# Zero products in another type and number, and the first tile of x in two parts

## Chip, cores and metric

The kernel runs on one core of one Trainium2 chip. The metric is the device time of one execution in microseconds (us). The engines go by the profile's names: PE (TensorE; its weight loads are PEld), DVE (VectorE), ACT (ScalarE), POOL (GpSimd) and SP (SyncE).

## Reference

The kernel computes a recurrent attention and, on its result, a gated feed-forward layer. q, k and v have 4 batches, 8 heads, 768 steps and a head dimension of 64; the layer has 512 inputs and 1536 hidden units.

```python
gamma = 1.0 - 2.0 ** (-5.0 - np.arange(H))
for t in range(S):
    state = gamma * state + k[t] (outer) v[t]          # per batch and head
    y[t] = scale * q[t] @ state
x = y.transpose(0, 2, 1, 3).reshape(B * S, H * D)      # 3072 x 512
gate = 1.0 / (1.0 + np.exp(-(x @ w_gate)))
out = (gate * (x @ w_val)) @ w_out
```

## The kernel before, in words

The 768 steps are cut into six chunks of 128. Inside a chunk the attention is a product of scores with a causal mask of decays; between chunks a state of 64x64 per head is carried. The four batches of a chunk are two *blocks* of two batches each, so there are twelve blocks (`i`, with `j` the batch within the block). The x of one chunk, 512 tokens of four batches by 512 features, is held as `xT`: 128 partitions by four row blocks (`kk`, one for each pair of heads) by 512 columns. The feed-forward layer of a chunk is 12 groups (`n1`) of 128 hidden units: four products over `kk` with `wg`, four with `wv`, a sigmoid on ACT, a product on DVE into `hT`; then `down` products with `wo`.

The order of the work is written out by hand: each engine takes its instructions in program order. Sums are held in eight banks (`bank()`), used in turn: a new one waits until the tile eight allocations ago has been read. Loads are issued by POOL in program order, apart from the first k and q (SP and ACT). Later chunks follow a hand-written plan; the change touches none of it but the name of the x tile.

The first chunk, where the change lies, runs so:

- POOL issues the loads of k, q and v for the first chunk (line 92; k of batch 0 and q of batch 0 come by SP and ACT in fp32), then the weights: `wg` and `wv` of the first 256 hidden units in two parts each (line 79), `kk` 0 and 1 first, and so on.
- DVE writes `zero` (line 135), a tile of 128x512 in bf16, and builds tables; among them `causal` (line 140, used for the decays; written anew at line 175, by `last_constants`, as a 0/1 table that POOL reads for `maskk`, line 184, much later).
- PE does `keep_on(11)`: eleven products of `zero` with itself into a bank that nobody reads (line 416). Four more `keep_on(1)` stand between later steps of the head.
- DVE and ACT cast k and q of batch 0 to bf16 (lines 161 and 162). For each block and batch PE then transposes k and q (line 311), ACT or DVE copies them to `kqT` (line 312), PE makes the scores (line 226), DVE masks them (line 318), PE makes y of the batch (line 326, in `first_y`), and an engine evicts y from its bank into 128 columns of `xT` (line 329): ACT for the first three batches, DVE for the last.
- ACT loads the table of the sigmoid (line 447), DVE writes the second `causal`.
- PE begins the feed-forward layer with `first_parts` (line 363): gate sums of `n1` 0 and 1 over `kk` 0 and 1, then over `kk` 2 and 3, and the same for val; then groups of up to 12 products (line 354), with the two first states in between (line 340, copied by DVE at line 343, cast at line 277).

The order of the eviction and the first products is

```python
    c = (2 * i + j) * C
    eng(xT[0][:, :, c:c + C], o)
...
    for lo in (0, 2):
        for n1, u in enumerate(us):
            for kk in range(lo, lo + 2):
                nc.tensor.matmul(u, w[:, kk, n1 * 128:(n1 + 1) * 128], xT[0][:, kk], start=(kk == 0), stop=(kk == KT - 1))
```

so that every product of the layer reads a tile that all four evictions have written.

Of the kernel before, what the change touches and what calls it, by code (L numbers as in the profile page):

```python
# [8 lines left out]
F32 = mybir.dt.float32  # L9
BF16 = mybir.dt.bfloat16  # L10
AX = mybir.ActivationFunctionType
ALU = mybir.AluOpType
# [3 lines left out]
def kernel(  # L16
# [12 lines left out]
    nc = tc.nc  # L29
# [3 lines left out]
    C = 128  # L33
    NT = S // C
    NP = H // 2
    KT = D_MODEL // 128
# [6 lines left out]
    const = ctx.enter_context(tc.tile_pool(name="const", bufs=1))  # L43
    wpool = ctx.enter_context(tc.tile_pool(name="wpool", bufs=1))
    ld = ctx.enter_context(tc.tile_pool(name="ld", bufs=2))
    at = ctx.enter_context(tc.tile_pool(name="at", bufs=2))
# [38 lines left out]
    def load_out(s):  # L85
        nc.gpsimd.dma_start(out=wo[:, s * 3:(s + 1) * 3, :],
                            in_=moe_w_out.rearrange("(n p) d -> p n d", p=128)[:, s * 3:(s + 1) * 3, :])
# [43 lines left out]
    tabsk = const.tile([128, NT, 2, H], F32, name="tabsk")  # L131
    taby = const.tile([128, NP, C], F32, name="taby")
    tabz = const.tile([128, NT, 2, NP], F32, name="tabz")
    zero = const.tile([128, 512], BF16, name="zero")
    nc.vector.memset(zero, 0.0)  # L135
    nc.vector.memset(lsc, math.log(scale))
    for h in range(H):
# [36 lines left out]
    def last_constants():  # L174
        nc.vector.tensor_scalar(causal, ahead, 0.0, None, op0=ALU.is_le)
# [13 lines left out]
    xT, sc, stA, stB, y, za, zz, zb = {}, {}, {}, {}, {}, {}, {}, {}  # L189

    def bank(shape, dt=F32):
        return pf.tile(shape, dt, tag="ff", name="ff")

    def half(e):
        return slice(e * D, (e + 1) * D)
# [4 lines left out]
    def new_kqT(i):  # L200
        kqT[i] = at.tile([128, 2, 2, NP, C], BF16, tag="kqT", name="kqT", bufs=2)
# [43 lines left out]
    def intra(i, j):  # L245
        for p in range(NP):
            for e in range(2):
                st = (stA, stB)[e ^ j][i, j]
                nc.tensor.matmul(y[i, j][half(e), p, :], vs[i][:, j * H + 2 * p + e, :], st[:, p, :],  # L249
                                 start=False, stop=True, skip_group_check=True)  # L250

    def y_out(i, j):
        t = i // 2
        if t not in xT:
            xT[t] = at.tile([128, NP, 512], BF16, tag="xT", name="xT")
        c = (i % 2 * 2 + j) * C
        nc.vector.tensor_tensor(xT[t][:, :, c:c + C], y[i, j], taby, op=ALU.mult)  # L257

    def state(i):
        zz[i] = bank([128, 2, NP, D])  # L260
# [7 lines left out]
    def new_za(i):  # L268
        za[i] = at.tile([128, 2, NP, D], F32, tag="za", name="za", bufs=4)
# [9 lines left out]
    def block(old, new):  # L279
        last = new is None or new >= NPAIR - 2  # L280
        if old is not None:
            new_y(old)
            inter(old)
        for j in range(2):
            if new is not None:
                scores(new, j)
        for j in range(2):
            if old is not None:
                intra(old, j)
        if not last:  # L290
            state(new)
        for j in range(2):
            if old is not None:
                y_out(old, j)
        for j in range(2):
            if new is not None:
                mask(new, j, 0)
                mask(new, j, 1)
        if not last:
            state_sum(new)  # L300
# [6 lines left out]
    def first_transpose(i, j, which, eng):  # L307
        x = (kn[i], qn[i])[which]
        tp = bank([128, NP, C], BF16)
        for p in range(NP):  # L310
            nc.tensor.transpose(tp[:, p, :], heads(x, j, p), ident)
        eng(kqT[i][:, which, j], tp)

    def first_scores(i, j):
        scores(i, j)
        for e, st in enumerate((stA, stB)):
            st[i, j] = at.tile([128, NP, C], BF16, tag=f"st{e}", name=f"st{e}", bufs=4)
            nc.vector.tensor_tensor(st[i, j], sc[i, j][e], decay[:, e], op=ALU.mult)

    def first_y(i, j, eng):  # L320
        if 0 not in xT:
            xT[0] = at.tile([128, NP, 512], BF16, tag="xT", name="xT")
        o = bank([128, NP, C])
        for p in range(NP):
            for e, st in enumerate((stA, stB)):
                nc.tensor.matmul(o[half(e), p, :], vs[i][:, j * H + 2 * p + e, :], st[i, j][:, p, :],
                                 start=(p == 0), stop=True, skip_group_check=True)
        c = (2 * i + j) * C
        eng(xT[0][:, :, c:c + C], o)  # L329

    def first_scaled(i, j, x):
        nc.gpsimd.tensor_tensor(entry(ks[i], j), x, tabs[:, :, 0].unsqueeze(2).to_broadcast([C, H, D]), op=ALU.mult)

    def first_state(i):
        z = bank([128, 2, NP, D])
        for j in range(2):
            for p in range(NP):
                for e in range(2):
                    n = j * H + 2 * p + e
                    nc.tensor.matmul(z[half(e ^ j), j, p, :], ks[i][:, n, :], vs[i][:, n, :],  # L340
                                     start=(j == 0 and p == 0), stop=True, skip_group_check=True)
        new_za(i)
        nc.vector.tensor_copy(za[i], z)
# [5 lines left out]
    def up_part(t, w, n1s, lo=0, hi=512):  # L349
        n = hi - lo  # L350
        u = bank([128, 512])
        for i, n1 in enumerate(n1s):
            for kk in range(KT):
                nc.tensor.matmul(u[:, i * n:(i + 1) * n], w[:, kk, n1 * 128:(n1 + 1) * 128], xT[t][:, kk, lo:hi],  # L354
                                 start=(kk == 0), stop=(kk == KT - 1))
        return u[:, :len(n1s) * n]

    def first_parts(w):
        us = [bank([128, 512]) for _ in range(2)]
        for lo in (0, 2):  # L360
            for n1, u in enumerate(us):
                for kk in range(lo, lo + 2):
                    nc.tensor.matmul(u, w[:, kk, n1 * 128:(n1 + 1) * 128], xT[0][:, kk], start=(kk == 0), stop=(kk == KT - 1))  # L363
        return us

    def gate_times_val(t, n1s, lo, hi, ps):
        n = hi - lo
        if t not in hT:
            hT[t] = ffn.tile([128, NFF, 512], BF16, tag="hT", name="hT", bufs=2)
        gs = ffn.tile([128, 512], F32, tag="gs", name="gs")  # L370
        g = gs[:, :len(n1s) * n]
        nc.scalar.activation(g, ps[0], AX.Sigmoid)  # L372
        nc.vector.tensor_tensor(hT[t][:, n1s[0]:n1s[-1] + 1, lo:hi], g.rearrange("p (i n) -> p i n", n=n),  # L373
                                ps[1].rearrange("p (i n) -> p i n", n=n), op=ALU.mult)

    def up(t, n1s, lo=0, hi=512):
        gate_times_val(t, n1s, lo, hi, [up_part(t, w, n1s, lo, hi) for w in (wg, wv)])
# [35 lines left out]
    def keep_on(n):  # L413
        u = bank([128, 512])
        for _ in range(n):
            nc.tensor.matmul(u, zero[:, :128], zero, start=True, stop=True)  # L416

    act, dve = nc.scalar.copy, nc.vector.tensor_copy  # L420

    new_kqT(0)
    new_kqT(1)
    keep_on(11)
    first_transpose(0, 0, 0, dve)
    first_transpose(0, 0, 1, act)
    later_constants()
# [1 line left out]
    first_scores(0, 0)  # L429
    first_transpose(0, 1, 1, act)  # L430
    first_transpose(1, 0, 0, act)
    keep_on(1)
    first_scores(0, 1)
    first_transpose(1, 0, 1, act)
    keep_on(1)
    first_scores(1, 0)
    first_transpose(1, 1, 0, act)
    later_exps()
    first_transpose(1, 1, 1, dve)
    keep_on(1)  # L440
    first_y(0, 0, act)
    first_scores(1, 1)
    first_y(0, 1, act)
    keep_on(1)
    first_y(1, 0, act)
    first_y(1, 1, dve)
    nc.scalar.preload_act_table(AX.Sigmoid)
    last_constants()
    first_scaled(0, 0, kf)
    first_scaled(0, 1, entry(kn[0], 1))  # L450
    load_gate_val(3)
# [4 lines left out]
    for n1, ps in enumerate(zip(first_parts(wg), first_parts(wv))):  # L456
        gate_times_val(0, (n1,), 0, 512, ps)
    for n1 in (2, 4):
        gates = [up_part(0, wg, (n1 + i,)) for i in range(2)]
        for i in range(2):  # L460
            gate_times_val(0, (n1 + i,), 0, 512, (gates[i], up_part(0, wv, (n1 + i,))))
        first_state(n1 // 2 - 1)
    load_out(0)
    load_out(1)
    load_kq(2)
# [35 lines left out]
    for j in range(2):  # L501
        y_out(2, j)
# [68 lines left out]
```

## Time and profile before

| | us |
|---|---|
| median of 4 runs | 228.64 (228.54 to 230.09) |
| the profiled execution | 228.73 |
| its span, first to last instruction | 227.0 |
| PE busy in the span | 219.9 |
| POOL busy | 104.9 |
| DVE busy | 111.2 |
| ACT busy | 71.8 |
| the 15 zero products on PE | 6.4 |
| first feed-forward product starts | 15.79 |

The profile shows one execution. The span is shorter than the execution by what lies around it. Busy shares are means over the whole span; where an engine stood still is read from the chain of work that ended last and from the timeline, which lists instructions by start, with the idle time before each and what ended it.

The chain says that of the span 92% is PE, 4% POOL and 2% DMA. POOL and DMA stand in it before 14.5 us alone; after 15.79 it is PE to the last copy.

### The profile page before, as it was taken

The page shows a single profiled execution, that of the slowest core. Times are in us where ns is not written, and L with a number is a line of the kernel's source. Part 1 is how long each engine was busy: PE and PEld are TensorE (multiplying, and loading weights), DVE is VectorE, ACT ScalarE, POOL GpSimd, SP SyncE. Part 2 cuts the span into 40 slices and gives each one's busy share as a digit, 9 for nine tenths or more (in the row PEclk, how much of TensorE's full clock was granted, in tenths as well). Part 3 has the DMA queues.
Part 4 walks back from the last instruction along what each step waited for, and adds up shares of the span by engine and source line. Part 5 has one row for each costly group of instructions (what it writes and reads, how often), then busy time and mean ns, then how long its engine had stood idle before and what let it go on. Part 6 is the DMA issues. An engine that isn't in the chain of part 4 may idle for free.

```text
span 227.0 us, 4324 instructions
## 1 busy us (share of the span) xinstructions
PE 219.9 (97%) x1767; PEld 116.9 (51%) x1767; DVE 111.2 (49%) x198; ACT 71.8 (32%) x120; POOL 104.9 (46%) x127
## 2 busy tenths in 40 slices
PE   7869999999999999999999999999999999999994
PEld 2534445558888555445445445445445444444443
DVE  6753653163954776735916634904443802333301
ACT  6674232336233212332321332321433321333221
POOL 8999969999849989089900081000000000000000
PEclk9999999999999999999999999999999999999999
DMA  9999999999999999999952799012600012100022
GB/s 128 152 174 195 189 199 168 162 210 196 150 133 148 146 179 187 180 137 102 101 84 87 161 123 87 3 46 95 137 3 0 3 46 92 49 1 0 0 95 92
DMA packets 103668, 25.19 MB, mean 111 GB/s; under 512 B 92640, under 2 KB 100704, under 8 KB 103648
## 3 DMA queue, kind: packets, MB, share of 16 engines
q0 software_dynamic: 80928, 13.90, 80.8%
q1 hardware_dynamic: 21536, 10.69, 20.4%
q10 hardware_dynamic: 1184, 0.33, 0.6%
q8 instruction: 14, 0.23, 0.4%
q14 instruction: 6, 0.05, 0.1%
HBM read 28.31 MB, written 6.29 MB: 152 GB/s over the span
## 4 chain that ended last, share of the span: by engine, by line
PE 92%; POOL 4%; DMA 2%; DVE 0%; issue 0%; POOLq 0%
PE ff L354 54%; PE ff L389 27%; PE ff L249 2%; PE ff L226 2%; DMA vs<-in_v_dram 2%; PE ff L363 2%; PE ff L242 2%; POOL kn L92 1%; PE ff L402 1%; POOL qn L92 1%; POOL vs L92 1%; PE ff L264 1%; PE ff L207 1%; PE ff L340 0%; DVE xT L329 0%
## 5 line engine op out<-in xcount | busy, mean ns | idle before, releaser
L373 DVE TENSOR_TENSOR hT<-gs,ff 128x512 bf16<-128x512 f32 x72 | 49.0, 686 | 63.2 <-PE ff L354 60.2
L354 PE MATMUL ff<-xT,wg 128*128 128x512 bf16 (+1 forms) x328 | 71.7, 348 | 0.0
L354 PE MATMUL ff<-xT,wv 128*128 128x512 bf16 (+1 forms) x328 | 71.7, 348 | 0.0
L372 ACT ACTIVATE gs<-ff 128x512 f32<-128x512 f32 x72 | 42.9, 597 | 83.6 <-PE ff L354 79.0
L389 PE MATMUL ff<-wo,hT 128*128 128x512 bf16 x276 | 62.2, 379 | 0.0
L354 PEld LDWEIGHTS <-wv 128*128 128x128 bf16 x328 | 32.1, 98 | 28.5
L354 PEld LDWEIGHTS <-wg 128*128 128x128 bf16 x328 | 31.4, 98 | 27.6
L389 PEld LDWEIGHTS <-hT 128*128 128x128 bf16 x276 | 26.2, 98 | 30.8 <-DVE hT L373 0.4
L393 ACT COPY ob<-ff 128x512 f32<-128x512 f32 x23 | 13.5, 585 | 58.7 <-PE ff L389 54.7
L232 DVE TENSOR_TENSOR st<-ff,maskk 128x512 bf16<-128x512 f32 x40 | 24.8, 682 | 6.4 <-PE ff L226 6.4
L257 DVE TENSOR_TENSOR xT<-ff,taby 128x512 bf16<-128x512 f32 x20 | 12.9, 686 | 29.6 <-PE ff L249 29.6
L218 POOL TENSOR_TENSOR ks<-kn,tabsk 128x1024 bf16<-128x1024 bf16 x8 | 15.9, 1988 | 0.0
L67 POOL DMA_DIRECT2D qn<-in_q_dram x20 | 15.4, 800 | 0.9 <-DMA wv<-in_moe_w_val_dram 0.6
L67 POOL DMA_DIRECT2D kn<-in_k_dram x20 | 15.2, 780 | 0.0
L515 POOL COPY held<-kqX 128x1 bf16<-128x1 bf16 x6 | 1.2, 208 | 28.4 <-DMA kqX<-qn 28.4
L57 POOL DMA_DIRECT2D vs<-in_v_dram x10 | 12.2, 1221 | 0.0
L63 POOL DMA_DIRECT2D kn<-in_k_dram x10 | 9.5, 946 | 0.9 <-issue 0.9
L63 POOL DMA_DIRECT2D qn<-in_q_dram x10 | 9.3, 928 | 0.0
L277 DVE TENSOR_TENSOR zb<-za,tabz 128x512 bf16<-128x512 f32 x10 | 8.0, 812 | 0.2
L416 PE MATMUL ff<-zero 128*128 128x512 bf16 x15 | 6.4, 565 | 1.2 <-DVE zero L135 1.2
L249 PE MATMUL ff<-st,vs 128*64 128x128 bf16 x160 | 6.4, 222 | 0.0
L79 POOL DMA_DIRECT2D wg<-in_moe_w_gate_dram x7 | 5.7, 834 | 0.0
(73 smaller groups left out, 121.2 us busy)
## 6 DMA issues: line engine op xcount, KB each, us to landing
out_dram<-ob SPq DMA_DIRECT2D x23, 256.0 KB, 2.2
vs<-in_v_dram POOLq DMA_DIRECT2D x10, 256.0 KB, 7.0
kn<-in_k_dram POOLq DMA_DIRECT2D x13, 128.0 KB, 5.1
qn<-in_q_dram POOLq DMA_DIRECT2D x13, 128.0 KB, 5.4
wo<-in_moe_w_out_dram POOLq DMA_DIRECT2D x4, 384.0 KB, 7.8
wg<-in_moe_w_gate_dram POOLq DMA_DIRECT2D x5, 256.0 KB, 6.1
wv<-in_moe_w_val_dram POOLq DMA_DIRECT2D x5, 256.0 KB, 6.7
kn<-in_k_dram POOLq DMA_DIRECT2D x20, 64.0 KB, 5.7
```

What stands on the lines that cost most here:

```text
L57: nc.gpsimd.dma_start(out=vs[i], in_=v[2 * h:2 * h + 2, :, t * C:(t + 1) * C, :].rearrange("b h s d -> s (b h) d"))
L63: nc.gpsimd.dma_start(out=tiles[i][:, 0:H], in_=src[0])
L67: nc.gpsimd.dma_start(out=dst[:, e], in_=pairs[:, 1 - e])
L218: nc.gpsimd.tensor_tensor(ks[i], kn[i], tabsk[:, i // 2].rearrange("s j h -> s (j h)").unsqueeze(2) .to_broadcast([C, 2 * H, D]), op=ALU.mult)
L232: nc.vector.tensor_tensor(st[i, j], sc[i, j][e], maskk[:, e ^ j], op=ALU.mult)
L249: nc.tensor.matmul(y[i, j][half(e), p, :], vs[i][:, j * H + 2 * p + e, :], st[:, p, :], start=False, stop=True, skip_group_check=True)
L257: nc.vector.tensor_tensor(xT[t][:, :, c:c + C], y[i, j], taby, op=ALU.mult)
L354: nc.tensor.matmul(u[:, i * n:(i + 1) * n], w[:, kk, n1 * 128:(n1 + 1) * 128], xT[t][:, kk, lo:hi], start=(kk == 0), stop=(kk == KT - 1))
L372: nc.scalar.activation(g, ps[0], AX.Sigmoid)
L373: nc.vector.tensor_tensor(hT[t][:, n1s[0]:n1s[-1] + 1, lo:hi], g.rearrange("p (i n) -> p i n", n=n), ps[1].rearrange("p (i n) -> p i n", n ...
L389: nc.tensor.matmul(o, hT[t][:, n1, b * C:(b + 1) * C], wo[:, n1, :], start=(n1 == 0), stop=(n1 == NFF - 1))
L393: nc.scalar.copy(ob, o)
```

## The change

The zero tile becomes 128x256 in fp32. `keep_on` multiplies 256 columns instead of 512. Five such products stand where eleven did, and the four single ones are gone.

The first chunk's x is held in two tiles, one with row blocks 0 and 1, one with 2 and 3; `x_of` finds the tile. Each eviction of the first chunk is made in two halves, one for each tile. ACT makes both for the first two batches; for the last two DVE makes the first half and ACT the second. x of the later chunks stays one tile, in two buffers of its own.

`last_constants`, the second `causal`, moves from before POOL's `first_scaled` calls to behind the second `first_state`.

```diff
-    zero = const.tile([128, 512], BF16, name="zero")
+    zero = const.tile([128, 256], F32, name="zero")
...
+    def new_xT(t, n=1):
+        xT[t] = [at.tile([128, NP // n, 512], BF16, tag=f"xT{n}", name="xT", bufs=2) for _ in range(n)]
+
+    def x_of(t, kk, lo=0, hi=512):
+        per = NP // len(xT[t])
+        return xT[t][kk // per][:, kk % per, lo:hi]
...
-    def first_y(i, j, eng):
+    def first_y(i, j, engs):
         if 0 not in xT:
-            xT[0] = at.tile([128, NP, 512], BF16, tag="xT", name="xT")
+            new_xT(0, 2)
...
-        eng(xT[0][:, :, c:c + C], o)
+        for g, eng in enumerate(engs):
+            eng(xT[0][g][:, :, c:c + C], o[:, 2 * g:2 * g + 2])
...
     def keep_on(n):
         u = bank([128, 512])
         for _ in range(n):
-            nc.tensor.matmul(u, zero[:, :128], zero, start=True, stop=True)
+            nc.tensor.matmul(u[:, :256], zero[:, :128], zero, start=True, stop=True)
...
-    keep_on(11)
+    keep_on(5)
     first_transpose(0, 0, 0, dve)
...
     first_transpose(1, 0, 0, act)
-    keep_on(1)
     first_scores(0, 1)
     first_transpose(1, 0, 1, act)
-    keep_on(1)
     first_scores(1, 0)
     first_transpose(1, 1, 0, act)
     later_exps()
     first_transpose(1, 1, 1, dve)
-    keep_on(1)
-    first_y(0, 0, act)
+    first_y(0, 0, (act, act))
     first_scores(1, 1)
-    first_y(0, 1, act)
-    keep_on(1)
-    first_y(1, 0, act)
-    first_y(1, 1, dve)
+    first_y(0, 1, (act, act))
+    first_y(1, 0, (dve, act))
+    first_y(1, 1, (dve, act))
     nc.scalar.preload_act_table(AX.Sigmoid)
-    last_constants()
     first_scaled(0, 0, kf)
...
         first_state(n1 // 2 - 1)
+    last_constants()
     load_out(0)
```

The products of `up_part` and `first_parts` read `x_of(t, kk, lo, hi)` in place of `xT[t][:, kk, lo:hi]`.

## Prediction

> **What bounds the kernel now.** I read the page's busy shares first, then the chain of work that ended last, then the timeline of the first 20 us.
>
> ```profile
> PE 219.9 (97%) x1767; PEld 116.9 (51%) x1767; DVE 111.2 (49%) x198; ACT 71.8 (32%) x120; POOL 104.9 (46%) x127
> ...
> PEclk9999999999999999999999999999999999999999
> ```
>
> PE is busy in 97% of the span, at a granted clock that never drops in the records. A change can gain only where PE stands still, or lose by making PE wait or run slower. The chain says where PE stood still:
>
> ```profile
> 9.29 5.16 DMA vs<-in_v_dram
> 14.45 0.04 issue
> 14.49 0.43 PE ff L326 x8
> 14.92 0.02 issue
> 14.95 0.70 DVE xT L329
> 15.65 0.14 issue
> 15.79 3.61 PE ff L363 x16
> 19.40 3.45 PE ff L354 x16
> ```
>
> Columns: start, length, what. Up to 14.45 the end is set by GpSimd's queue of loads, whose last early one, v of batch 3, lands at 14.45; PE's own work before that is not on the chain. Then come the last y block (14.49 to 14.92), its eviction on DVE, and from 15.79 PE without a break to 223.8. So all that this change can gain lies between 14.92 and 15.79: 0.87 us. All that it can lose is a later 15.79, or slower products after it.
>
> The timeline of the head (start, length, engine, line, operation, and in brackets the idle time and what ended it):
>
> ```profile
> 1.19 4.87 PE L416 MATMUL ff<-zero 128*128 128x512 bf16 x11 [1.19 <-DVE zero L135]
> ...
> 5.62 0.62 ACT L162 CAST qn<-qf 128x512 bf16<-128x512 f32 x1 [0.54 <-DMA qf<-in_q_dram]
> 5.86 0.63 PE L311 MATMUL ff<-ident,kn 128*128 128x128 bf16 x4
> 6.29 0.52 PE L311 MATMUL ff<-ident,qn 128*128 128x128 bf16 x4
> 6.65 0.39 PE L311 MATMUL ff<-ident,kn 128*128 128x128 bf16 x4
> ...
> 7.98 4.02 DVE L318 TENSOR_TENSOR st<-ff,decay 128x512 bf16<-128x512 f32 x6 [0.33 <-ACT kqT L312]
> ...
> 12.80 1.29 DVE L318 TENSOR_TENSOR st<-ff,decay 128x512 bf16<-128x512 f32 x2 [0.47 <-PE ff L226]
> ...
> 14.95 0.69 DVE L329 CAST xT<-ff 128x512 bf16<-128x512 f32 x1 [0.85 <-PE ff L326]
> ```
>
> Two things are to be seen. The eleven zero products start every 0.42 us ((5.86 - 1.19) / 11), the ones from 15.79 every 0.22 (3.61 / 16): PE works at half rate at first, though the granted clock shows nothing of it. Four transposes take 0.63, then 0.52, then 0.39, so the rate doubles near 6.5, after 5.3 us of unbroken work. Second, beside the loads runs a chain with little slack: cast of q (ends 6.24), transposes, scores, DVE's six masks without a pause from 7.98, and the last two, which end at 14.09. The last y could start then; it waits for v until 14.45. That slack is 0.36 us.
>
> **The change part by part.**
>
> *The eviction.* Today 128x512 on DVE takes 0.69. Then DVE takes two of four row blocks, 128x256, and the first four gate products read only these. The nearest rows are the two evictions of the kernel's end (of PSUM too, but into f32):
>
> ```profile
> 222.53 0.42 DVE L409 COPY ob<-ff 128x256 f32<-128x256 f32 x1 [8.32 <-PE ff L402]
> ...
> 223.20 0.27 ACT L406 COPY ob<-ff 128x128 f32<-128x128 f32 x1 [1.40 <-PE ff L402]
> 223.87 0.29 DVE L409 COPY ob<-ff 128x128 f32<-128x128 f32 x1 [0.92 <-PE ff L402]
> ```
>
> I take 0.42, the same shape: 0.69 - 0.42 = 0.27 us saved, and PE starts at 15.52. Bounds: a half no shorter than the 128x128 row's 0.29 saves 0.40; one as long as the whole saves nothing. The hard limit is the 0.87 above. As built, ACT's half waits for DVE's half of the same bank, so the halves follow each other: ACT from about 15.42, for a length between 0.27 (128x128) and 0.58 (its 128x512 rows), by the middle to 15.8. The fifth gate product needs it at 15.52 + 4 x 0.215 = 16.38: covered by 0.5 us. Queued behind ACT's half is the Sigmoid table load (1.28, now at 14.81); it would end at 17.1, and the first sigmoid finds its bank full at about 17.0 (today 17.28). Its 0.1 us delay meets no one: gs and hT are next needed by bank reuse microseconds later. The blocks before: DVE's half of the third block runs 14.2 to 14.6, before the last is ready at 14.92, and ACT's four short copies of the first two blocks have until then (today ACT idles 0.34 before its third).
>
> *What is late next.* The weights. The first gate part (issued 10.15, 4.7 us to landing) is there at 14.9 and the second at 15.3. The second part of val lands at 17.7 and is loaded by PE at 18.15 today, 17.9 then. The next gate columns land at 18.7; PE loads them at 19.02, then 18.75. This cover is used up at 0.3 us of gain; more would be given back there. The rest has over 0.6: q of block 2 lands at 38.4 for transposes at 39.1, the third part of w_out at 40.3 for 41.1.
>
> *The four single zero products.* They stand at 8.55, 9.46, 11.26 and 13.18, each 0.38 us. Behind the first the next weight load waits 0.26 for an ACT copy; behind the others PE itself waits 0.46 for a copy, 0.29 and 0.19 for v. Taking them away gains nothing; PE only waits longer. Their four banks leave the ring of eight, which makes the reused banks older, never younger. What their going may do to PE's rate is a rival below.
>
> *The eleven become five in fp32.* No row shows an fp32 product. From below, 256 columns at the pace of the bf16 rows take 0.21 us: the five end at 2.3. From above, as if each of four bytes took a pass of its own with its weight load (151 ns here) hidden behind nothing: 4 x (0.21 + 0.15) = 1.46, and they end at 8.5. No row is nearer, so I take the middle, 0.84: end at 5.4. The point that decides is known: the transposes of k need 0.43 before those of q, which can't start before 6.29 in any case. So an end by 5.86 costs nothing, and up to 6.22 the 0.36 us of slack at v hides it. At 8.5 the cost is 2.27 us.
>
> The Trainium skill, "FP8 and Floating Point Precision", section "TensorE Precision Notes", says that true fp32 takes four passes through the array. By that my estimate would be 4 x 0.21 = 0.85 a product and the sum the same; no run here shows it yet.
>
> *The causal table.* 0.52 us of DVE moves from 15.55, where DVE then idles until 19.07, to behind the second state copy at 28.1. Queued behind it there are zb (needed on PE at 48.2) and a product hT after which DVE idles 0.84. GpSimd reads the table at 34.4, covered by 5.8 us. Zero. x of the later tiles keeps two buffers: zero.
>
> **The sum.** The profiled execution took 228.73 (span 227.0 and 1.7 around it): 228.73 - 0.27 = 228.46. It is 0.09 above the median of 228.64, so the forecast is **228.4**.
>
> **Rivals.**
>
> *PE runs at half rate when the dense products begin (slower).* Place: the gate products from 15.5. For it: the rate rose only after 5.3 us of unbroken work; in the changed kernel that work is other work, may be shorter, and is followed by a pause of about 0.4 until q comes; and the four zeros that filled the waits are gone. Without them PE has some 1.5 us of transposes and 1.5 of scores and y between 7 and 15. Against it: no pause of PE in that stretch is over 1 us. Price: if the climb takes 5.3 us again, half of it, 2.65, and about 0.35 for slower transposes, scores and y on the masks' chain after its slack: 228.4 + 3.0 = 231.4. It decides from 2.8 us at half rate on (1.4 lost).
>
> Against this change speaks a rule of "TensorE: Matmul & The Clock Gate", section "Part 4: PE-mode transpose": transposes do not count as work for the clock. Its "Part 1: The HAM clock gate" asks for a busy window of 3.4 us to speed up and an idle one to slow down. If transposes don't count, the longest pause without zeros is 2.0 us, from 5.4 to 7.5, so the fast state, once reached, would hold. But the five products must then fill a window alone, in 4.2 us where the eleven had 4.7; by this rule a miss costs about 1.7, and the sum is some 230.1.
>
> *The fp32 products are long.* Their price is anywhere up to 1.46; at that end 228.64 - 0.27 + 2.27 = 230.6. Half of this case lies above 0.5%.
>
> *The gain is not there (it does not do what it says).* DVE's half costs nearly the whole, or a weight load takes over the wait: 228.7. For it: the cover at 18.7 is thin; against it, the 0.42 row has the very shape.
>
> **How the numbers follow.** Forecast 0.62; no gain 0.10; long fp32 products 0.08; half rate 0.18; a gain by something that I do not see 0.02. About 0.5% (1.14 us) is what a measurement of this kernel can tell from no change; the forecast's gain is within it, and even the hard limit of 0.87 is. Faster 0.02, same 0.62 + 0.10 + 0.04 = 0.76, slower 0.18 + 0.04 = 0.22. The range goes from the hard limit, 228.64 - 0.87 = 227.8, to the long end of the fp32 products, 230.7, and leaves out the half rate, 0.18.
>
> **What would show it.** Right: five zero products that end before 5.9; scores at 7.5; the last y at 14.49; DVE's 128x256 copy at 0.42 and the first gate product near 15.5; sixteen of them in about 3.5 us; chain PE from there. Wrong: gate products 0.42 apart (half rate), DVE's first mask later than 8.3 (long fp32), a PE wait for weights near 18.7.

## The result, and the profile after

The changed kernel takes 230.27 us in the median of 48 executions (228.33 to 231.50), the kernel before 228.81 in 74. The ratio is 1.0043, with a 95% interval from 1.0029 to 1.0057 (the ratios here and below are those on record; they are not the quotient of the two medians, which is 1.0064 here). That is slower, clear of the noise though small, where 228.4 and no measurable change were forecast. The executions of both kernels differ in one thing that must be told to understand these numbers: the mean granted clock of PE over the execution. I call an execution one *with a half clock stretch* where that mean is 0.993 or less; a stretch of 3.4 us at half rate lowers the mean by 0.0075 (half of 3.4 in a span of 227). The changed kernel had one in 43 of 48 executions, the kernel before in 16 of the 95 that ran beside the experiments. (For the 74 above no clock is on record; 20 of them took more than 229.9.) The five changed ones with no such stretch took 228.33, 228.47, 228.50, 228.54 and 229.27. Three of the 43 took no longer (228.50, 228.54 and 228.59, each with one stretch of 3.4 us), so such a stretch does not always cost time; where it lay in these three is not on record.

The profiled execution took 231.19. From its page, the shares and the granted clock in 40 slices:

```profile
span 229.4 us, 4318 instructions
...
PE 221.8 (97%) x1762; PEld 119.4 (52%) x1762; DVE 112.8 (49%) x199; ACT 72.1 (31%) x123; POOL 104.9 (46%) x127
...
PEclk9976999999999999999999999999999999999999
```

The third and fourth slice (11.5 to 22.9 us) show 7 and 6 where before all 40 showed 9. Next, the chain of work that ended last, 13 to 24 us:

```profile
9.28 5.05 DMA vs<-in_v_dram
14.33 0.04 issue
14.37 0.66 PE ff L334 x7
15.03 0.02 issue
15.05 0.44 DVE xT L338
15.49 0.14 issue
15.62 6.27 PE ff L372 x16
```

The chain has the same members as before. The last y takes 0.66 in place of 0.43, its eviction 0.44 in place of 0.70, and the sixteen products of `first_parts` 6.27 in place of 3.61. That is +2.66 on a start that is 0.17 earlier (15.62 for 15.79): 2.5, and the span has grown by 2.4 (229.4 - 227.0). After these products the two traces run alike.

The granted clock stretch by stretch (columns: stretch, its length, PE's busy time with its instructions, granted clock, DMA share, GB/s), first the changed kernel, then the one before:

```profile
7.38:10.79 3.41, 2.46 (x40) 1.00 2.50 151
10.79:14.20 3.41, 2.14 (x38) 1.00 2.40 160
14.20:17.61 3.41, 2.62 (x13) 0.50 1.44 192
17.61:21.03 3.42, 3.42 (x9) 0.50 1.45 196
```

```profile
6.57:9.98 3.41, 2.72 (x38) 1.00 2.56 151
9.98:13.40 3.42, 2.72 (x42) 1.00 3.03 150
13.40:16.81 3.41, 2.02 (x22) 1.00 1.47 188
```

The clock fell to half at 14.20 and came back at 21.03. Before the fall PE was busy for 2.46 and 2.14 us of two stretches of 3.41; in the kernel before, over the two stretches that follow its own rise at 6.57, for 2.72 and 2.72, and nothing fell, not even after a third stretch with 2.02 busy. So the rate did rise in the changed kernel, and it was lost again ahead of the dense products.

### The profile page after: what moved, and what is told of

Read it like the earlier page. It is cut to its first block, busy times and chain, and to the rows that moved or that the text cites. A ratio compares the mean times of both kernels' runs of the same rounds, so it can differ in the third digit from the quotient of the medians.

```text
span 229.4 us, 4318 instructions
## 1 busy us (share of the span) xinstructions
PE 221.8 (97%) x1762; PEld 119.4 (52%) x1762; DVE 112.8 (49%) x199; ACT 72.1 (31%) x123; POOL 104.9 (46%) x127
## 4 chain that ended last, share of the span: by engine, by line
PE 92%; POOL 4%; DMA 2%; issue 0%; DVE 0%; POOLq 0%
PE ff L363 53%; PE ff L398 26%; PE ff L372 3%; PE ff L249 2%; PE ff L226 2%; DMA vs<-in_v_dram 2%; PE ff L242 2%; POOL kn L92 1%; PE ff L411 1%; POOL qn L92 1%; POOL vs L92 1%; PE ff L272 1%; PE ff L207 1%; PE ff L349 0%; PE ff L334 0%
## 5 line engine op out<-in xcount | busy, mean ns | idle before, releaser
L363 PE MATMUL ff<-xT,wg 128*128 128x512 bf16 (+1 forms) x328 | 71.7, 348 | 0.0
L363 PE MATMUL ff<-xT,wv 128*128 128x512 bf16 (+1 forms) x328 | 71.7, 348 | 0.0
L363 PEld LDWEIGHTS <-wv 128*128 128x128 bf16 x328 | 32.1, 98 | 28.5
L363 PEld LDWEIGHTS <-wg 128*128 128x128 bf16 x328 | 31.4, 98 | 27.6
L285 DVE TENSOR_TENSOR zb<-za,tabz 128x512 bf16<-128x512 f32 x10 | 9.4, 949 | 0.2
L425 PE MATMUL ff<-zero 128*128 128x256 f32 x10 | 4.6, 650 | 1.2 <-DVE zero L135 1.2
```

## The experiments

Theory A: the four single zero products kept PE busy enough between 7 and 14 us; without them the clock falls. Theory B: the five fp32 products are to blame. Theory C: the eviction in halves is.

| run | median us (range) | with a half clock stretch |
|---|---|---|
| e1: before, no single products | 231.03 (230.14 to 231.64) | 8 of 8 |
| e2: before, five fp32 in front | 228.69 (228.51 to 230.49) | 2 of 12 |
| e3: x in two parts, zeros as before | 228.55 (228.18 to 230.12) | 1 of 12 |
| e4: changed, four single ones back | 228.76 (228.26 to 230.43) | 2 of 12 |
| e5: changed, transposes in their place | 228.71 (228.30 to 229.38) | 1 of 11 |
| e6: changed, first two back | 228.76 (228.17 to 231.23) | 5 of 12 |
| e7: changed, last two back | 228.71 (228.24 to 229.94) | 2 of 12 |
| e8: x in two parts, all waits filled | 228.56 (228.36 to 229.57) | 0 of 11 |
| e9: x in two parts, waits filled but for one | 228.39 (228.31 to 228.94) | 0 of 12 |
| e10: x in two parts, nothing in front | 229.61 (229.22 to 230.41) | 0 of 12, but a late rise |
| e11: before, single ones moved behind y | 230.01 (228.55 to 231.10) | 8 of 12 |

**e1, the single products alone.** All four `keep_on(1)` taken out of the kernel before.

```diff
     first_transpose(1, 0, 0, act)
-    keep_on(1)
     first_scores(0, 1)
```

> The kernel before without its four single zero products (8.55 to 13.18); all else as before. Theory A (too little PE work between 7 and 14 us lets the clock fall to half just before the dense products): slow as the changed kernel, median near 230.3, a granted clock under 1 in most runs. Theory B (the five fp32 products raise the clock less surely than eleven bf16 ones): no different from before, 228.8, most runs with no half clock. Theory C (the eviction in halves costs the time): 228.8.

231.03; ratio to before 1.0085 (1.0057 to 1.0113). All eight executions had a half clock stretch. The chain of its profile:

```profile
14.62 0.66 PE ff L326 x8
15.28 0.02 issue
15.30 0.69 DVE xT L329
16.00 0.14 DVE causal L175
16.14 0.00 issue
16.14 6.20 PE ff L363 x16
```

The same 6.20 for sixteen products, with eleven bf16 products in front and x whole. Theory A holds; B and C expected no difference here. The clock stretches of this profile:

```profile
4.33:7.74 3.41, 2.57 (x29) 1.00 2.25 145
7.74:11.16 3.42, 2.05 (x31) 1.00 2.45 149
11.16:14.57 3.41, 2.99 (x36) 0.50 2.20 163
14.57:17.98 3.41, 2.48 (x13) 0.50 1.44 192
17.98:21.40 3.42, 3.42 (x10) 0.50 1.45 196
```

Here the rate rose at 4.33 and fell at 11.16, again 6.83 later, after a stretch with 2.05 busy; full rate came back at 21.40.

**e2, the front alone.** Five fp32 products in front of the kernel before, the four single ones kept in bf16 (their tile is written a little later, behind other small tables).

```diff
-    keep_on(11)
+    keep_on4(5)          # 256 columns of a zero tile in fp32
```

> The kernel before with five fp32 products of 256 columns in place of the eleven, the four single ones kept in bf16; x undivided. Theory A: as before, 228.8. Theory B: slow, near 230.3. Theory C: 228.8.

228.69, ratio 1.0001 (0.9979 to 1.0024). Theory B falls.

**e3, x in two parts alone.** The changed kernel with all fifteen bf16 products.

```diff
-    zero = const.tile([128, 256], F32, name="zero")
+    zero = const.tile([128, 512], BF16, name="zero")
...
-    keep_on(5)
+    keep_on(11)
...
+    keep_on(1)
     first_scores(0, 1)
```

> The changed kernel with all fifteen bf16 zero products of before: only x in two parts, the eviction in halves and the later causal table are new. Theory A and B: the forecast's gain of 0.27 to 0.30 alone, so 228.5 where the clock stays up, with as many runs at half clock as before. Theory C: 230 or more.

228.55, ratio 0.9989 (0.9968 to 1.0011). Its chain:

```profile
9.28 5.16 DMA vs<-in_v_dram
14.44 0.04 issue
14.49 0.43 PE ff L334 x8
14.92 0.02 issue
14.95 0.43 DVE xT L338
15.38 0.14 issue
15.52 3.61 PE ff L372 x16
19.13 3.46 PE ff L363 x16
```

This is the chain that the prediction worked out: last y at 14.49 as before, eviction 0.43 (0.42 was forecast), products at 15.52. The gain of 0.27 is there in this profile; in the medians it is 0.18 (228.73 for the kernel before beside it), and the interval of the ratio holds no change. Theory C, which asks for 230 or more, falls.

**e4, the single products put back** into the changed kernel, in fp32 with 128 columns.

```diff
+    keep_on(1, 128)
     first_scores(0, 1)
```

> The changed kernel with four single zero products put back at their old places, fp32 with 128 columns, about as long as the bf16 ones with 512. Theory A: most runs at full clock, median 228.5. Theory B: as the changed kernel, 230.3. Theory C: 230.3.

228.76, ratio 0.9994 (0.9969 to 1.0020). The loss of the change is gone. Its profiled execution took 229.16 at full clock, and shows the other thing that spreads the times. The chain from 13 to 24 us, and two of the waits (who waited for whom: us, times, longest):

```profile
12.93 6.71 DMA wg<-in_moe_w_gate_dram
19.64 0.05 issue
19.68 3.63 PE ff L363 x16
```

```profile
PEld L363 <- DMA wg<-in_moe_w_gate_dram: 0.8, 1, 0.8
PEld L372 <- DMA wv<-in_moe_w_val_dram: 0.7, 1, 0.7
```

Here the gate weights of the next two groups landed at 19.64, not at 18.7, and their first load waited 0.8; the second part of val was late too (the load waited 0.7). The products that follow the first sixteen (L363) start at 19.68, in e3 at 19.13: 0.55 later. The profile of e7 (229.16) shows the same, with the gate weights at 19.62 and the second part of val at 18.55 in place of 17.7. In the kernel before, 16 of the 95 executions lie at 229.0 or above without a half clock stretch; that these are late weights too is argued, not shown.

**e5, is it products or any work?** Four transposes of a zero tile, 128 columns each, at each of the four places.

```diff
+    turn_on()            # 4 x nc.tensor.transpose(u[:, p, :], zero16, ident)
     first_scores(0, 1)
```

> The changed kernel with four transposes of a zero tile (128 columns each, together about as long on PE as one single zero product was) at each of the four old places. Theory A1 (any PE work holds the clock): as with the single products put back, 228.7, most executions at full clock. Theory A2 (transposes do not count as work for the clock): as the changed kernel, 230.3, most executions with a half clock stretch.

228.71, ratio 0.9985 (0.9964 to 1.0006). One of 11 executions had a half clock stretch, where 43 of 48 had one without these transposes: transposes hold the clock as products do. The Trainium skill, "TensorE: Matmul & The Clock Gate", section "Part 4: PE-mode transpose", says that full clock does not engage for transposes and that they do not count as busy in the same way; this run speaks against it. (The trace records them as MATMUL of 128x128 with the identity; whether the mode that the page speaks of was on, it does not say.)

**e6 and e7, two of the four.** The changed kernel with only the first two, or only the last two, put back (edit as in e4).

> The changed kernel with only the first two single products put back (near 8.4 and 9.4). If the clock is judged over single stretches of 3.4 us and the last one, 10.8 to 14.2, fell too low: still slow, 230.3. If it is judged over the whole 6.8 us: half way, 229.5, about half of the executions with half clock.

> The changed kernel with only the last two single products put back (near 11.2 and 13.1). If single stretches are judged: 228.7 to 229.3, well under half of the executions with half clock. If the whole 6.8 us: as with the first two alone, 229.5.

5 of 12 and 2 of 12 with a half clock stretch, against 43 of 48 with none and 2 of 12 with all four. Two products more than halve the share. Whether the clock is judged over one stretch or two these runs do not settle: 5 and 2 of 12 are too near each other.

**e11, is it the pause ahead of the dense products?** A rival that the chain suggests: PE stands still from 14.9 to 15.6. The kernel before without its single products, with three behind the last y.

```diff
     first_y(1, 1, dve)
+    keep_on(3)
```

> The kernel before without its four single products, but with three behind the last y, in the pause ahead of the dense products. If that pause makes the clock fall: back to 228.8. If the thin stretch between 7 and 14 does (theory A, the falls at 14.2 and 11.2 in the profiles): slow still, 230 to 231, most executions with a half clock stretch.

230.01 beside 228.92 for the kernel before, ratio 1.0024 (0.9994 to 1.0053): the times alone do not settle it. But 8 of 12 had a half clock stretch, where 6 of the 29 of the kernel before beside it had one. The profile:

```profile
5.19:8.60 3.41, 2.50 (x31) 1.00 2.44 152
8.60:12.01 3.41, 2.12 (x35) 1.00 2.75 148
12.01:15.43 3.42, 2.75 (x41) 0.50 1.90 172
15.43:18.84 3.41, 3.41 (x9) 0.50 1.44 193
18.84:22.25 3.41, 3.41 (x17) 1.00 1.45 196
```

The fall at 12.01 is three us ahead of that pause. The pause isn't the cause of this fall. In its share of half clock stretches the kernel lies between e1 and before; why four of its executions escaped, and none of e1's eight, is not shown.

**e10, the front taken to its end.** e3 without `keep_on(11)`.

> x in two parts with the four single products and no zero products in front. The rival of the prediction (the clock is not up when the dense products begin, because the front work is too short) taken to its end: if the front products are what raises the clock, the head runs at half rate and the dense products begin so, median 230.5 to 231.5, half clock or no rise before 15 in most executions. If transposes and scores raise it themselves a stretch or two later: 228.6 to 229.2.

229.61, ratio 1.0022 (1.0000 to 1.0044): between the two expectations. PE's part of the timeline shows the rate:

```profile
9.35 0.61 PE L226 MATMUL ff<-kqT 64*128 64x128 bf16 x8
9.89 0.61 PE L319 MATMUL ff<-ident,qn 128*128 128x128 bf16 x4
...
11.17 0.40 PE L226 MATMUL ff<-kqT 64*128 64x128 bf16 x8 [0.42 <-ACT kqT L320]
11.50 0.40 PE L319 MATMUL ff<-ident,kn 128*128 128x128 bf16 x4
```

Eight scores take 0.61 up to 9.35 and 0.40 from 11.17, so transposes, scores and two single products raise the clock by themselves, only later: the rises in the profiles with a front lie between 3.9 and 7.4. The recorded mean clock can't show it: it counts as full whatever lies ahead of the first rise. The price is on the masks' chain: the last two masks run from 13.69 to 14.98, the last y at 15.02, products at 16.01 instead of 15.52.

**e8 and e9, the waits filled.** On e3, more single products in PE's waits (the edit shown is that of e9). e8 has one, three, two and two at the old places, two ahead of the last y and three behind it; e9 one, two, two and two, none ahead and two behind.

```diff
     first_transpose(1, 0, 1, act)
-    keep_on(1)
+    keep_on(2)
     first_scores(1, 0)
...
     first_y(1, 1, (dve, act))
+    keep_on(2)
```

> x in two parts with the eleven bf16 products of before, and the waits of PE filled: one, three, two and two single products at the four old places, two ahead of the last y and three behind it. Theory A: no execution with half clock in the head, median 228.4, none near 230.2. If the few half clock stretches of before have another cause: as many as before, about one in six, near 230.2. If the added products delay real work: 228.7 or more at full clock.

> x in two parts with the eleven bf16 products, one, two, two and two single products at the old places and two behind the last y, none ahead of it. Theory A: no execution with half clock in the head; gate products from 15.5 and a median of 228.4, below the 228.55 of x in two parts with four single ones and below the 228.7 of before. If filling gains nothing over four single ones: one execution in eight near 230.2.

Neither had a half clock stretch in 11 and 12 executions. The kernel before, beside them, had 7 of 35 and 6 of 29. e8 took 228.56 (0.9986, 0.9965 to 1.0006): its products were a little in the way, the two ahead of y above all (y began at 14.59, with v there at 14.17). e9 took 228.39 beside 228.92, ratio 0.9976 (0.9960 to 0.9992): a little faster than the kernel before. Its chain:

```profile
14.35 0.41 PE ff L334 x8
14.76 0.16 issue
14.92 0.38 PE ff L425
15.30 0.07 issue
15.38 3.61 PE ff L372 x16
```

The two products behind y end at 15.30, just ahead of the first real one. That one starts 0.14 earlier than in e3 because v landed at 14.30 in this execution, not at 14.44; it is no gain of the filling. What the filling adds to e3 in time is not shown: the two ratios' intervals overlap, and 0 of 12 is close to e3's 1 of 12.

## Why the prediction was wrong, point by point

- **Where the kernel is bound** was right: v landing, last y, eviction, then PE. The change moved the time inside that chain alone.
- **The eviction** was right in kind and size: 0.43 for 0.42, products at 15.52 (e3's profile), ACT's half at 15.40 for 0.37.
- **The fp32 products** were right: the page of the changed kernel's groups shows ten records for five products, and the timeline

```profile
1.19 4.63 PE L425 MATMUL ff<-zero 128*128 128x256 f32 x10 [1.19 <-DVE zero L135]
5.62 0.63 PE L319 MATMUL ff<-ident,kn 128*128 128x128 bf16 x4
```

  has their starts done with by 5.62: (5.62 - 1.19) / 5 = 0.89 a product, for 0.84 by the middle of my bounds. No cost (e2), and the scores began at 7.35.
- **What is late next**, the weights at 18.7, was the right suspect: in single executions they land at 19.6 and the products behind them start about 0.5 late (e4, e7). I took one execution's landing for a constant.
- **The causal table and the later x tiles** cost nothing that a run shows: e3 has both and is not slower.
- **The four single zero products are the step that failed.** "Taking them away gains nothing; PE only waits longer" is right as a count of work, but it puts their worth as holders of the clock at nothing, and leaves that to a rival with 0.18. Without them 43 of 48 executions lose part of the clock (8 of 8 in e1); with them back it is 2 of 12 (e4). What I held against it, that no pause of PE is over 1 us, doesn't bear on it: the clock fell with PE busy 2.14 us of 3.41, no pause over 0.7 long. The rule of the Trainium skill that I drew on for this, an idle window of 3.4 us before a fall ("TensorE: Matmul & The Clock Gate", section "Part 1: The HAM clock gate"), is not what the runs show; its window of 3.4 us is (steps 6.83 and 10.24 apart, two and three times 3.41). The rival named the missing zero products and the outcome, but priced the wrong event: a rise that comes late because the front is shorter. The rise came (7.38), and e2 clears the front. What I missed was the fall.
- **The price** came out near, 231.4 for 231.19 in the profiled execution, but by luck: it was half of a climb of 5.3 us of work, and no such climb exists in the runs. With the same five fp32 products in front the rise came anywhere from 4.07 (e5) to 7.38. What was lost is half of the 5.41 us from 15.62 to 21.03. The median, 230.27, is lower; the recorded means (0.976 to 0.993) say that the half clock stretches were one to three windows of 3.4 us, but where they lay in the executions that were not profiled is not shown.
- **The sign that I passed over** stood in the numbers of before: of its four executions one took 230.09, about 1.5 us above the others. 16 of 95 executions had a half clock stretch, and all of these took 229.9 or more. The kernel before was itself close to the fall, and a change that takes PE work from the head moves that share, not a fixed cost.

The range of 227.8 to 230.7 held the median, by the allowance for long fp32 products, so for a wrong reason.

That the missing zero products let the clock fall is shown (e1, e4). What stays open is how much work in a stretch holds the clock. Busy time doesn't order the cases alone (it fell after 2.05 to 2.14, and did not in the kernel before after 2.02 over 13.40 to 16.81).

## What to carry to other kernels

Work that computes nothing can still hold PE's rate: before idle-time products are taken out as free, look at how busy PE stays for some 7 us ahead of the first dense stretch, and try the removal alone, over many executions. One execution at 1.5 us above the others can be a second level with its own cause, as here; ask what it is, since a change can move the share of executions on it. Filling PE's waits with products that end before the awaited data (e9), together with the eviction in halves, made a kernel 0.24% faster than the one before; the eviction alone (e3) is within the noise, and products that end after the data has come delay real work (e8).

## What the runs showed of the hardware

- The granted clock fell to half although PE was never idle for more than 0.7 us in the two stretches ahead (three profiles, with PE busy for 2.05 to 2.14 us of the last 3.41). Falls came 6.83 us after the rise in three profiles (7.38 and 14.20; 4.33 and 11.16; 5.19 and 12.01), and full rate came back 6.83 or 10.24 later. Rises lie anywhere from 3.9 to 7.4 in kernels with a front, and from 4.07 to 7.38 where the front is the same five fp32 products, so the steps don't follow the kernel's start.
- Transposes hold the clock (e5: 1 of 11 against 43 of 48), and the head's own work raises it without a front (e10: eight scores take 0.61 at 9.35 and 0.40 at 11.17).
- One fp32 product of 256 columns is recorded as two and takes 0.89 at half rate, about what two bf16 products of 512 columns take there (0.42 each).
- The record shows the granted clock as 1.00 ahead of its first change, while products are 0.42 apart: the rate there is read from the starts of products.
